# LayerNorm transposes by DMA, a third score bank, a later start of the q and k transposes by DMA, loads on the GpSimd queue, and another order of the first batch

## The chip, the cores and the metric

The kernel runs on one core of a Trainium2 chip. The core has a tensor engine for matrix products (PE, with its weight loads PEld), a vector engine (DVE), an activation engine (ACT), a general engine (GpSimd, POOL) and a queue engine that only starts transfers (SyncE, SP). Each runs its own list of instructions strictly in order and waits for the others by semaphores. Sixteen DMA engines move data; SP, ACT and POOL can each hand them work. The metric is the device time of one execution in microseconds (us); lower is better.

## What is computed

Attention over 8 batches of 12 heads, 448 tokens and 64 columns, with q and k normalised by their root mean square and scaled by g_q and g_k; its output is the input of a LayerNorm and of a two-layer network of width 3072 with a residual:

```python
q_n, k_n = rmsnorm(q, g_q), rmsnorm(k, g_k)
attn = softmax(q_n @ k_n.T / 8)
x = (attn @ v) -> (batch, 448, 768)
xn = (x - mean(x)) / sqrt(var(x) + 1e-6) * g_ln
out = x + relu(xn @ w_ch1) @ w_ch2
```

## The kernel before

Heads go in pairs, six to a batch, 48 in all (pair 0 to 47). Loads and preparation go by **units**: units 0 to 3 are batch 0 (one, one, two and two pairs), and each later batch has three units of two pairs (units 4, 5, 6 are batch 1; unit 7 begins batch 2). A unit's q, k and v come by nine DMAs (L117 and L125) into one of two buffers `qkv`.

The preparation of a unit is cut into pieces that have letters: `a`, `c` square k and q on ACT (L196), `d`, `e` sum the squares on DVE (L199), `g` takes the reciprocal root on ACT (L56, L57), `i` multiplies k by g_q g_k on POOL (L205), `j` rounds it to fp16 on ACT (L213), `k` takes the rest on DVE (L216), `l` scales q on DVE (L63), `m` doubles it, `v`, `w`, `z` convert v on POOL (L262, L268). Then q and k are transposed: up to unit DMA_UNIT by PE into the PSUM bank `tr` or `psQ` and copied by DVE (`K` and `Q` with the pair's number, L290 to L312), from there on by DMA transposes on SP's queue (pieces `x` and `y`, L235 to L248).

`S p.i` is one of seven score steps of a pair: a product of 448 columns on PE (L326, in the last step L329 and L330) and its exponential on ACT (L332), over two PSUM banks. `V p.i` is the matching step of the product with v (L355, L357), and after the seventh DVE divides (L370 to L377). `T` takes LayerNorm's statistics (L499), `A` joins them, `N t` centres one tile of 128 tokens (L519), `X t` transposes it by six PE products and one copy (L546 to L551), `R` is the scale.

The network of a batch is a list of chunks of six products each: 24 of the first layer (psH, L564, with a ReLU on ACT, L566) and, for each tile of 128 tokens, eight of the second (psC, L577, added on DVE, L581). Even batches have three tiles (48 chunks); odd batches also take the left-over tokens of two batches, four tiles (56 chunks).

Batch 0's attention is written out by hand in the table ORDER, which sets the order of every engine there, weight loads included (`W0` to `W4`, converted from fp32 to fp16 by DMAs on POOL's queue, L473 and L478; `L u` is the load of unit u). From then on `run_rest` emits the network of batch b chunk by chunk and lays the attention steps of batch b + 1 between them evenly, so that they end `tail` chunks before the network does; the rest of the chunks has LayerNorm's pieces of batch b + 1 between them. The preparation of a unit is spread over the steps between `st` and `e` in `attention`, the load of the unit after next comes at step `e`.

Of the kernel before, what the change touches and what calls it, by code (L numbers as in the profile page):

```python
# [8 lines left out]
FP32 = mybir.dt.float32  # L9
FP16 = mybir.dt.float16  # L10
INT32 = mybir.dt.int32
ALU = mybir.AluOpType
# [16 lines left out]
DVE_KG, POOL_HI, POOL_DUP, ACT_Q = (0, 1), (1, 2, 3, 4), (1, 2, 4, 5), (0, 1)  # L29
# [6 lines left out]
b0 c0 e0 a0 gq0 d0 b1 i0 G j0 z0 a1 k0 c1 l0 i1 gk0 m0 d1 K0 Q0 e1 b2 g1 a2 l1 j1 d2 m1 S0.0  # L36
S0.1 k1 S0.2 S0.3 L4 W0 L5 K1 c2 e2 S0.4 W1 V0.0 i2 S0.5 Q1 g2 l2 V0.1 j2 S0.6 S1.0 m2 S1.1
S1.2 b3 V0.2 z2 k2 V0.3 S1.3 a3 c3 S1.4 K2 V0.4 V0.5 Q2 V0.6 V1.0 V1.1 S1.5 i3 d3 S1.6 e3 S2.0
V1.2 T0 S2.1 K3 S2.2 S2.3 V1.3 V1.4 z3 S2.4 Q3 W2 V1.5 V1.6 S2.5 S2.6 V2.0 S3.0 g3 S3.1 V2.1
j3 S3.2 W3 W4 S3.3 k3 V2.2 l3 m3 S3.4 K4 b4 Q4 V2.3 a4 V2.4 S3.5 V2.5 V2.6 S3.6 Q5 V3.0 S4.0  # L40
S4.1 K5 c4 V3.1 V3.2 i4 S4.2 S4.3 V3.3 V3.4 V3.5 d4 V3.6 S4.4 S4.5 e4 S4.6 j4 V4.0 V4.1 S5.0
T1 V4.2 k4 g4 S5.1 V4.3 S5.2 V4.4 S5.3 b5 V4.5 l4 z4 m4 G2 L6 S5.4 V4.6 S5.5 a5 V5.0 V5.1 K6
# [29 lines left out]
class _Fast:  # L72


    def __init__(self, ctx, tc, sh, q, k, v, g_ln, w1, w2, out):
        self.g_ln = g_ln
# [26 lines left out]
        self.rr = fix.tile([128, 2, 7 * B * NPAIR], FP32, name="rr_all", tag="rr_all")  # L103
# [23 lines left out]
    def load_first(self):  # L127
# [44 lines left out]
    def pieces(self, u):  # L172
# [9 lines left out]
        def begin():  # L182
# [4 lines left out]
            c["rf"] = self.rr[:, :, o:o + g]  # L187
# [13 lines left out]
        def root(n=slice(0, 2)):  # L201
            _rsqrt(nc, c["rf"][:, n], c["ssq"][:, n], c["rt"][:, n], D * 1e-6)

        def kg():
            (nc.vector if u in DVE_KG else nc.gpsimd).tensor_tensor(  # L205
                out=c["t"][1], in0=c["t"][1],
                in1=sh.gprod.unsqueeze(1).broadcast_to([128, g, D]), op=ALU.mult)
# [11 lines left out]
        def qn():  # L219
            if u < DMA_UNIT:  # L220
                _scaled(nc, c["qn"][:, :, 0], c["t"][0], c["rf"][:, 0])
                return
            x, r = c["t"][0], c["rf"][:, 0]
# [61 lines left out]
    def trans_k(self, p):  # L285
# [3 lines left out]
        kT, ps = self.kU[0][:, 960 * (p % 2):960 * (p % 2) + 960], self.tr  # L289
# [7 lines left out]
    def trans_q(self, p):  # L297
# [5 lines left out]
        qT = self.qU[0][:, p % 2].rearrange("p e s -> p (e s)")  # L303
# [9 lines left out]
        kT = self.kU[0][:, 960 * (p % 2):960 * (p % 2) + 960]  # L313
        self.prs[p] = dict(q=qT, main=kT[:, 192:960], left=kT[:, 0:192])

    def scores(self, p, i):
# [6 lines left out]
        ps = self.ps_s.tile([128, 512], FP32, tag="psS", name="psS")  # L323
# [4 lines left out]
        else:  # L328
# [4 lines left out]
                             scale=self.rr[:, 1, g:g + 1], bias=EXP_BIAS)  # L333
# [53 lines left out]
    def first_attention(self):  # L387
# [7 lines left out]
        for x in ORDER:  # L395
# [7 lines left out]
            elif x == "G2":  # L403
                nc.vector.tensor_scalar(out=gln, in0=gln, scalar1=XS, scalar2=None, op0=ALU.mult)
            elif key == "W":
# [18 lines left out]
    def attention(self):  # L424
# [3 lines left out]
        for u in range(4, nu):  # L428
            p, m = UNIT_PAIR[u], UNITS[u][2]
            st = max(7 * (p - 2 - m) + 2, last + 1, 7 * nb0)  # L430
            e = max(7 * (p - 2) - 1, st + 5)
            pieces = ["bai", "d", "c", "e", "j", "gv", "k", "l", "m", "w", "x", "y"]
            k = len(pieces) - 2
            if u < nu - 2 and f"L{u + 2}" not in done:
                todo.setdefault(e, []).append(lambda u=u: self.load_unit(u + 2))
# [66 lines left out]
    def ln_ops(self, b):  # L502
# [13 lines left out]
        def norm(t):  # L516

            c["xn", t] = self.p_m.tile([128, DM], FP16, tag="xn", name="xn", bufs=3)
# [14 lines left out]
    def ln_list(self, b):  # L533
# [3 lines left out]
        return [call("A", "N0", "N1", "N2", "R")] + [  # L537
            call(f"X{t}", *([f"N{t + 3}"] if t + 3 < n else [])) for t in range(n)]

    def ln_trans(self, b, xn, t):  # L540
        nc, sh = self.nc, self.sh
        if t == 0:
            self.xnT = self.p_m.tile([128, NDC, 512], FP16, tag="xnT", name="xnT")
        ps = self.ps_m.tile([128, NDC, 128], FP16, tag="mlp", name="psX")
# [3 lines left out]
        if b == 0 and t < 2:  # L548
# [75 lines left out]
    def run_rest(self):  # L624
        steps, mark, upto = self.steps, self.mark, self.upto
        tail = 10
# [25 lines left out]
    def flag(self):  # L652
# [5 lines left out]
        good = self.p_m.tile([128, n], FP32, tag="xn", name="good", bufs=3)  # L658
# [5 lines left out]
        nk = self.rr.shape[2]  # L664
        nc.vector.tensor_scalar(out=good[:, 0:nk], in0=self.rr[:, 1], scalar1=sh.gmax,
# [127 lines left out]
def kernel(  # L793
# [21 lines left out]
    gg = sh.w2[:, 0, 0:4 * D].bitcast(FP32).rearrange("p (n d) -> p n d", n=2)  # L815
    nc.scalar.dma_start(gg[:, 0], g_q.unsqueeze(0).broadcast_to([128, D]))
    nc.scalar.dma_start(gg[:, 1], g_k.unsqueeze(0).broadcast_to([128, D]))
    sh.gprod = const.tile([128, D], FP32, name="gprod")
    nc.vector.tensor_tensor(out=sh.gprod, in0=gg[:, 0], in1=gg[:, 1], op=ALU.mult)
    sh.gmax = const.tile([128, 1], FP32, name="gmax")  # L820
    nc.vector.tensor_reduce(out=sh.gmax, in_=sh.gprod, axis=AX.X, op=ALU.max,
                            apply_absolute_value=True)
# [47 lines left out]
```

## Time and profile before

| | |
|---|---|
| median of three runs | 649.29 us (648.17 to 650.2) |
| the profiled execution | 649.09 us, of which the span from first to last instruction is 647.3 |
| PE busy | 594.3 us (92% of the span) |
| ACT, DVE, POOL busy | 362.7, 293.0, 103.1 us |
| granted PE clock, mean | 0.973 |
| moved by DMA | 73.12 MB, on average 113 GB/s |

A busy PE isn't a PE at its peak: products overlap, and a row's time is the time until its results stand. What a product costs is read from the distance between starts.

### The profile page before, as it was taken

To read this page: it belongs to the slowest core of one execution; us is meant where nothing else is said; L and a number is where in the kernel's file an instruction comes from. 1 tells how busy PE (TensorE), PEld (TensorE's weight loads), DVE (VectorE), ACT (ScalarE), POOL (GpSimd) and SP (SyncE) were. 2 spreads that over 40 slices of the span, in tenths; PEclk is the share of its full clock that TensorE was granted. 3 is DMA by queue.
4 is the path that set the end of the run, shared out by engine and by line. 5 is a ranking of instruction groups with operands and counts; after the bars stand their busy time and mean duration, and the time that the engine had idled before them with its cause. 6 is when DMAs were issued, how large, how long until landed. Compare 5 with 4: busy or idle time off the path is not lost.

```text
span 647.3 us, 11504 instructions
## 1 busy us (share of the span) xinstructions
PE 594.3 (92%) x4506; PEld 349.6 (54%) x4506; DVE 293.0 (45%) x633; ACT 362.7 (56%) x673; POOL 103.1 (16%) x116
## 2 busy tenths in 40 slices
PE   2873957999999999999999999999999999999995
PEld 1552534565556666665556666665556666654563
DVE  5795504573425625672434625582443621380011
ACT  5974736644874368635874288626874277314300
POOL 2942310220210202220220111210221100000000
PEclk9996879899999999999999999999999999999998
DMA  8999985554255354564255355455243230010011
GB/s 231 246 220 221 200 178 120 140 140 157 62 141 131 94 130 119 110 151 113 55 133 139 90 132 119 113 140 126 66 107 79 71 62 4 25 50 0 2 50 53
DMA packets 149836, 73.12 MB, mean 113 GB/s; under 512 B 99728, under 2 KB 144784, under 8 KB 149776
## 3 DMA queue, kind: packets, MB, share of 16 engines
q1 hardware_dynamic: 140960, 62.82, 39.4%
q0 software_dynamic: 8528, 9.44, 8.6%
q8 instruction: 37, 0.61, 0.4%
q14 instruction: 23, 0.19, 0.1%
q10 hardware_dynamic: 288, 0.07, 0.0%
HBM read 52.36 MB, written 11.01 MB: 98 GB/s over the span
## 4 chain that ended last, share of the span: by engine, by line
PE 74%; DVE 8%; SPq 7%; DMA 4%; ACT 3%; issue 2%; POOL 0%; ACTq 0%; DVEq 0%; POOLq 0%
PE psH L564 32%; PE psC L577 25%; PE psS L326 7%; PE oA L355 4%; SPq L125 4%; DVE xn L519 3%; DMA qkv<-in_v_dram 2%; PE oB L357 1%; SPq L245 1%; SPq L117 1%; DVE stat L499 1%; PE psX L546 1%; DVE khl L216 1%; ACT E L332 1%; PE psS L329 1%
## 5 line engine op out<-in xcount | busy, mean ns | idle before, releaser
L564 PE MATMUL psH<-xnT,w 128*128 128x512 f16 (+1 forms) x1152 | 250.4, 358 | 0.0
L332 ACT ACTIVATE E<-psS,rr_all 128x448 f16<-128x448 f32 x336 | 207.8, 632 | 71.1 <-PE psS L326 64.6
L577 PE MATMUL psC<-w,hT 128*128 128x384 f16 x1344 | 241.8, 326 | 1.6 <-DVE x L581 1.6
L566 ACT ACTIVATE hT<-psH 128x384 f16<-128x384 f32 (+1 forms) x192 | 105.0, 547 | 132.0 <-PE psH L564 130.8
L577 PEld LDWEIGHTS <-hT 128*128 128x128 f16 x1344 | 124.1, 98 | 72.7 <-issue 2.2
L564 PEld LDWEIGHTS <-w 128*128 128x128 f16 x1152 | 106.0, 99 | 85.1 <-issue 4.7
L326 PE MATMUL psS<-qU,kU 128*128 128x448 f16 x288 | 104.3, 365 | 17.7 <-DMA qU<-qn 10.5
L355 PEld LDWEIGHTS <-E 128*128 128x128 f16 x1008 | 71.6, 99 | 63.9 <-ACT E L332 11.8
L205 POOL TENSOR_TENSOR qkv<-qkv,gprod 128x896 f32<-128x896 f32 x21 | 43.7, 2082 | 325.6 <-issue 253.0
L355 PE MATMUL oA<-v,E 128*128 128x65 f16 x864 | 68.0, 196 | 5.6 <-ACT E L332 5.2
L581 DVE SCALAR_TENSOR_TENSOR x<-psC,rs_all,x 128x384 f32<-128x384 f32 x48 | 29.5, 617 | 85.7 <-PE psC L577 85.1
L199 DVE TENSOR_REDUCE ssq<-khl 128x14 f32<-128x896 f32 (+1 forms) x25 | 26.2, 1048 | 80.1 <-ACT khl L196 80.0
L370 DVE RECIPROCAL rec_all<-oA 128x6 f32<-128x6 f32 x48 | 9.3, 194 | 98.3 <-PE oA L355 98.1
L357 PE MATMUL oB<-v,E 128*128 128x65 f16 x288 | 52.6, 195 | 0.1
L326 PEld LDWEIGHTS <-kU 128*128 128x128 f16 x288 | 28.6, 100 | 36.5 <-issue 17.4
L63 DVE SCALAR_TENSOR_TENSOR qn<-qkv,rr_all 128x256 f16<-128x256 f32 (+2 forms) x81 | 26.9, 393 | 19.9 <-ACT rr_all L57 19.9
L199 DVE TENSOR_REDUCE ssq<-qn 128x14 f32<-128x896 f32 (+1 forms) x25 | 26.1, 1045 | 20.4 <-ACT qn L196 20.4
L357 PEld LDWEIGHTS <-E 128*128 128x128 f16 x336 | 33.0, 98 | 0.6 <-DVE xl L377 0.4
L216 DVE TENSOR_TENSOR khl<-qkv,khl 128x896 f16<-128x896 f32 x21 | 22.8, 1088 | 10.9 <-ACT khl L213 10.9
L372 DVE TENSOR_TENSOR x<-oA,rec_all 128x384 f32<-128x384 f32 x48 | 26.8, 558 | 1.5
L499 DVE BATCH_NORM_STATS2 stat<-x 128x6 f32<-128x256 f32 x72 | 26.1, 415 | 0.7
L262 POOL CAST v<-qkv 128x768 f16<-128x768 f32 x21 | 17.4, 828 | 35.6 <-PE oB L357 19.6
(87 smaller groups left out, 356.9 us busy)
## 6 DMA issues: line engine op xcount, KB each, us to landing
qkv<-in_k_dram SPq DMA_DIRECT2D x21, 384.0 KB, 3.4
qkv<-in_q_dram SPq DMA_DIRECT2D x21, 384.0 KB, 3.9
qkv<-in_v_dram SPq DMA_DIRECT2D x21, 384.0 KB, 4.2
out_dram<-x SPq DMA_DIRECT2D x20, 384.0 KB, 2.5
w<-in_moe_w_ch_dram POOLq DMA_DIRECT2D x3, 1536.0 KB, 20.3
w<-in_moe_w_ch_dram POOLq DMA_DIRECT2D x2, 2304.0 KB, 45.2
qU<-qn SPq DMA_TRANSPOSE x100, 2.4
out_dram<-x SPq DMA_DIRECT2D x8, 192.0 KB, 2.3
```

The source lines that it names most:

```text
L199: nc.vector.tensor_reduce(out=c["ssq"][:, n], in_=c["sq", n], axis=AX.X, op=ALU.add)
L205: (nc.vector if u in DVE_KG else nc.gpsimd).tensor_tensor(out=c["t"][1], in0=c["t"][1], in1=sh.gprod.unsqueeze(1).broadcast_to([128, g, D] ...
L216: nc.vector.tensor_tensor(out=c["khl"][:, :, 1], in0=c["t"][1], in1=c["khl"][:, :, 0], op=ALU.subtract)
L326: nc.tensor.matmul(ps[:, 0:S], c["main"][:, ts(i, 128)], q[:, ts(h, S)], start=True, stop=True)
L332: nc.scalar.activation(out=c["E"][:, i], in_=ps[:, 0:S], func=AFT.Exp, scale=self.rr[:, 1, g:g + 1], bias=EXP_BIAS)
L355: nc.tensor.matmul(oA[:, t, cs], E[:, i, ts(t, 128)], rhs, start=(i == 0 and t == 0), stop=(i == 6 and t == 2))
L357: nc.tensor.matmul(oB[:, cs], E[:, i, 320:448], rhs, start=(i == 0), stop=(i == 6))
L499: nc.vector.bn_stats(out=self.st[b][:, t, 6 * s:6 * s + 6], in_=x[:, 256 * s:256 * s + 256])
L564: nc.tensor.matmul(ps[:, 0:N], sh.w1[:, dc, ts(f, 128)], xnT[:, dc, 0:N], start=(dc == 0), stop=(dc == NDC - 1))
L566: nc.scalar.activation(out=hT[:, f, 0:N], in_=ps[:, 0:N], func=AFT.Relu)
L577: nc.tensor.matmul(ps[:, 0:384], hT[:, f, ts(t, 128)], sh.w2[:, f, ts(g, 384)], start=(f == 0), stop=(f == NFF - 1))
L581: nc.vector.scalar_tensor_tensor(out=x[:, ts(g, 384)], in0=ps[:, 0:384], scalar=self.rs[:, b, t:t + 1], in1=x[:, ts(g, 384)], op0=ALU.mult ...
```

## The change

- ORDER is rewritten and ends with batch 0; the preparation of unit 5 is no longer in it, but between the chunks of batch 0's network. On POOL `W0` stands ahead of unit 1's `j` and `m`, which stood ahead of it.
- The first transfers of k are started on ACT's queue, those of g_q and g_k on SP's. Their product is made in unit 0's piece `i`, and its maximum at `G2`. Unit 2's piece `i` goes from POOL to DVE, unit 5's `m` from POOL to DVE. The reciprocal roots of q and k go to separate tiles, by two instructions in place of one.
- DMA_UNIT is 7 in place of 5: units 5 and 6 (pairs 8 to 11) are transposed by PE.
- From pair 13 on every third score step takes the bank `tr`.
- The load of the unit after next comes one step later, and from unit 9 on (16 units) it is started by POOL.
- LayerNorm's `X` is a DMA transpose of 128 x 768 on SP for batches 1 to 7 (25 tiles), with all of LayerNorm's pieces emitted at once and `tail` 13 in place of 10.

```diff
-DVE_KG, POOL_HI, POOL_DUP, ACT_Q = (0, 1), (1, 2, 3, 4), (1, 2, 4, 5), (0, 1)
+DVE_KG, POOL_HI, POOL_DUP, ACT_Q = (0, 1, 2), (1, 2, 3, 4), (1, 2, 4), (0, 1)
...
-T3 V5.2 V5.3 S5.6 V5.4 V5.5 Q6 V5.6 S6.0 S6.1 S6.2 S6.3 T5 V6.0 z5 A N0 V6.1 V6.2 d5 N1 S6.4
-c5 V6.3 V6.4 i5 j5 X0 S6.5 X1 N2 e5 X2 k5 S6.6 V6.5 g5 l5 m5 x5 V6.6 R y5
+V5.3 V5.4 V5.5 Q6 V5.6 S6.0 S6.1 S6.2 S6.3 T5 S6.4 V6.0 A V6.1 N0 V6.2 N1 V6.3 S6.5 V6.4 X0
+S6.6 V6.5 X1 N2 X2 R V6.6
-DMA_UNIT = 5
+DMA_UNIT = 7
...
+for n, eng in ((0, nc.sync), (1, nc.scalar)):
+    main(eng, n, 0)
+    left(eng, n)
...
+eng = self.nc.sync if u < 9 else self.nc.gpsimd
...
+if p > UNIT_PAIR[DMA_UNIT] and (7 * p + i) % 3 == 2:
+    ps = self.ps_tr.tile([128, 512], FP32, tag="tr", name="psS3")
+else:
+    ps = self.ps_s.tile([128, 512], FP32, tag="psS", name="psS")
...
-e = max(7 * (p - 2) - 1, st + 5)
+e = max(7 * (p - 2) - 1 if u >= DMA_UNIT else 7 * (p - 1) + 1, st + 5)
...
-todo.setdefault(e, []).append(lambda u=u: self.load_unit(u + 2))
+todo.setdefault(e + 1, []).append(lambda u=u: self.load_unit(u + 2))
...
-return [call("A", "N0", "N1", "N2", "R")] + [
-    call(f"X{t}", *([f"N{t + 3}"] if t + 3 < n else [])) for t in range(n)]
+return [call("A", "N0", "N1", "X0", "N2", "X1", *(["N3"] if n > 3 else []), "X2",
+             *(["X3"] if n > 3 else []), "R")]
...
+if b:
+    nc.sync.dma_start_transpose(self.xnT[:, :, ts(t, 128)], xn)
+    return
...
-tail = 10
+tail = 13
```

ACT at the end of batch 0's attention, before. `khl<-qkv`, `qn<-qkv` are the squares and the rounding of unit 5, `xnT` the two copies of LayerNorm, `hT` the network's first ReLU:

```order
L332 ACTIVATE E<-psS,rr_all 128x448 x5
L196 ACTIVATE khl<-qkv 128x896
L332 ACTIVATE E<-psS,rr_all 128x448 x6
L196 ACTIVATE qn<-qkv 128x896
L213 ACTIVATE khl<-qkv 128x14x64
L549 COPY xnT<-psX 128x6x128
L332 ACTIVATE E<-psS,rr_all 128x448
L549 COPY xnT<-psX 128x6x128
```

The same place now:

```order
L344 ACTIVATE E<-psS,rr_all 128x448 x13
L571 COPY xnT<-psX 128x6x128
L344 ACTIVATE E<-psS,rr_all 128x448
L571 COPY xnT<-psX 128x6x128
L57 ACTIVATE stat<-stat 128x3
L58 ACTIVATE rs_all<-stat 128x3
L588 ACTIVATE hT<-psH 128x384
L201 ACTIVATE khl<-qkv 128x896
L588 ACTIVATE hT<-psH 128x384
L201 ACTIVATE qn<-qkv 128x896
L588 ACTIVATE hT<-psH 128x384
L222 ACTIVATE khl<-qkv 128x14x64
```

Unit 5's three instructions moved from ahead of the exponentials and of the copies that the network's first product needs to places behind the network's first three ReLUs.

SP at the end of batch 1's attention, before: the load of a unit, its predecessor's transposes of k and q, then the first stores of batch 0's result.

```order
L117 DMA qkv<-in_q_dram 128x4x192
L125 DMA qkv<-in_q_dram 64x2x64 x2
L117 DMA qkv<-in_v_dram 128x4x192
L125 DMA qkv<-in_v_dram 64x2x64 x2
L235 DMA_TRANSPOSE kU_112<-khl 128x12x128
L238 DMA_TRANSPOSE kU_112<-khl 128x2x64 x2
L245 DMA_TRANSPOSE qU_114<-qn 128x4x128 x3
L248 DMA_TRANSPOSE qU_114<-qn 128x2x64 x2
L605 DMA out_dram<-x 128x384
```

The same place now:

```order
L244 DMA_TRANSPOSE kU_107<-khl 128x12x128
L247 DMA_TRANSPOSE kU_107<-khl 128x2x64 x2
L254 DMA_TRANSPOSE qU_109<-qn 128x4x128 x3
L257 DMA_TRANSPOSE qU_109<-qn 128x2x64 x2
L564 DMA_TRANSPOSE xnT<-xn 128x6x128 x4
L627 DMA out_dram<-x 128x384
```

LayerNorm's four transposes stand behind the unit's own transposes and ahead of the stores, and the load is gone from this queue. On POOL it now stands between one unit's conversion of v and the next unit's piece `i` (L214):

```order
L271 CAST v_111<-qkv 128x12x64
L277 CAST vl<-qkv 64x2x64 x2
L118 DMA qkv<-in_k_dram 128x4x192
L126 DMA qkv<-in_k_dram 64x2x64 x2
L118 DMA qkv<-in_q_dram 128x4x192
L126 DMA qkv<-in_q_dram 64x2x64 x2
L118 DMA qkv<-in_v_dram 128x4x192
L126 DMA qkv<-in_v_dram 64x2x64 x2
L242 MEMSET kU_108 128x2x64
L214 TENSOR_TENSOR qkv<-qkv,gprod 128x896
```

Before, the conversion was followed by the next unit's L205 directly.

More of the change, by code (lines that the diff above doesn't have):

```diff
@@ L201, in root @@
         def root(n=slice(0, 2)):
-            _rsqrt(nc, c["rf"][:, n], c["ssq"][:, n], c["rt"][:, n], D * 1e-6)
+            nc.scalar.activation(c["rt"][:, n], c["ssq"][:, n], AFT.Ln, bias=D * 1e-6)
+            for i in range(2)[n] if isinstance(n, slice) else (n,):
+                nc.scalar.activation(c["r", i], c["rt"][:, i], AFT.Exp, scale=-0.5)
         def kg():
+            if u == 0:
+                nc.vector.tensor_tensor(out=sh.gprod, in0=sh.gg[:, 0], in1=sh.gg[:, 1], op=ALU.mult)
             (nc.vector if u in DVE_KG else nc.gpsimd).tensor_tensor(
@@ L404, in first_attention @@
                 nc.vector.tensor_scalar(out=gln, in0=gln, scalar1=XS, scalar2=None, op0=ALU.mult)
+                gmax = self.sh.gmax
+                nc.vector.tensor_reduce(out=gmax, in_=self.sh.gprod, axis=AX.X, op=ALU.max,
+                                        apply_absolute_value=True)
+                nc.vector.tensor_scalar(out=gmax, in0=gmax, scalar1=1.0 / K_MAX, scalar2=None,
+                                        op0=ALU.mult)
             elif key == "W":
@@ L547, in ln_trans @@
                              start=(dc == 0), stop=(dc == NDC - 1))
-        if b == 0 and t < 2:
+        if t < 2:
             nc.scalar.copy(out=self.xnT[:, :, ts(t, 128)], in_=ps)
```

65 lines of the change are left out of this document (30 added, 35 removed).

## The prediction

> **What bounds the kernel now.** I read the page's span and busy times first, then a table of stretches, then each engine's rows in order of time.
>
> ```profile
> span 647.3 us, 11504 instructions
> 0.00:45.00 45.00, 27.51 (x294) 17.28 (x295) 34.02 (x66) 35.66 (x68) 23.95 (x33) 1.00 1.02 234
> 45.00:66.60 21.60, 8.55 (x81) 5.09 (x78) 12.57 (x27) 9.22 (x17) 4.11 (x5) 0.67 1.22 221
> 66.60:150.00 83.40, 71.28 (x516) 42.48 (x514) 40.64 (x86) 45.78 (x87) 16.63 (x19) 0.90 0.74 155
> 150.00:228.50 78.50, 78.31 (x572) 44.33 (x571) 34.42 (x74) 46.62 (x83) 12.05 (x12) 1.00 0.44 112
> 228.50:293.50 65.00, 63.74 (x530) 39.95 (x528) 35.70 (x78) 43.02 (x83) 11.15 (x12) 1.00 0.56 125
> ```
>
> The columns are length, then busy time of PE, PEld, DVE, ACT and POOL, granted clock, DMA share and GB/s. There are two kernels in one. From 150 us on PE is hardly ever idle and has its full clock: only less PE work helps there. Before that PE is idle for 17.5 us to 45, for 13 us to 66.6 and for 12 us to 150, with a clock of 0.67 and 0.90 in the last two; there the waits decide. I follow the largest.
>
> ```profile
> 50.25 0.95 ACT L196 ACTIVATE khl<-qkv 128x896 f32<-128x896 f32 x1 [5.31 <-DMA qkv<-in_k_dram]
> 58.59 0.88 POOL L262 CAST v<-qkv 128x768 f16<-128x768 f32 x1 [12.96 <-DMA qkv<-in_v_dram]
> 60.47 2.07 POOL L205 TENSOR_TENSOR qkv<-qkv,gprod 128x896 f32<-128x896 f32 x1
> 62.57 0.95 ACT L213 ACTIVATE khl<-qkv 128x896 f16<-128x896 f32 x1 [5.42 <-POOL qkv L205]
> 63.43 0.78 ACT L549 COPY xnT<-psX 128x768 f16<-128x768 f16 x1
> 66.43 2.13 PE L564 MATMUL psH<-xnT,w 128*128 128x384 f16 x6
> PE psS L326 <- DMA qU<-qn: 10.5, 2, 6.5
> PE oA L355 <- ACT E L332: 10.3, 4, 4.7
> ```
>
> Unit 5's data are late because the weight DMAs fill the engines (share 1.22). But nothing of batch 0 needs unit 5: ACT merely stands in order behind its square (5.31 us) and its rounding (5.42 us), which waits for POOL's L205, which stands behind the conversion of v, which waits for v. So the exponentials and the xnT copies are late, PE waits 10.3 us, and the network starts at 66.4. After that PE waits another 10.5 us for two DMA transposes of q, and starts again at about half clock (the six products at 66.43 take 2.13).
>
> **Prices.** From distances between starts, at full clock:
>
> ```profile
> 609.42 31.21 PE psC L577 x192
> 277.71 0.35 PE L326 MATMUL psS<-qU,kU 128*128 128x448 f16 x1
> 277.90 0.26 PE L355 MATMUL oA<-v,E 128*128 128x65 f16 x3
> 278.02 1.14 PE L577 MATMUL psC<-w,hT 128*128 128x384 f16 x6
> 290.76 0.50 PE L546 MATMUL psX<-id,xn 128*128 128x128 f16 x6
> 291.10 1.14 PE L577 MATMUL psC<-w,hT 128*128 128x384 f16 x6
> ```
>
> 192 products of 384 columns in 31.21 us make a chunk of six 0.975; the first layer with three tiles has the same width. A score product is 0.19, a value step 0.12; the last value step of a pair is twice as wide in columns, estimated at 0.2. One LayerNorm tile on PE is 0.34, so 0.057 a transpose, and a `K` or `Q` of seven 0.40.
>
> **Batch 0 and the start of the network.** With unit 5 out of ORDER, ACT goes on after the five exponentials that end at 44.9. The next bound is pair 6's transposes.
>
> ```profile
> 42.18 2.76 ACT L332 ACTIVATE E<-psS,rr_all 128x448 f16<-128x448 f32 x5
> 47.91 0.61 DVE L312 COPY qU<-tr 128x896 f16<-128x896 f16 x1
> 52.32 0.20 DVE L370 RECIPROCAL rec_all<-oA 128x6 f32<-128x6 f32 x1 [3.81 <-PE oA L355]
> 56.85 1.93 DVE L519 SCALAR_TENSOR_TENSOR xn<-x,stat,gln 128x768 f16<-128x768 f32 x2
> ```
>
> That chain ran beside the long wait and stays: Q6's copy ends at 48.5. ACT then has seven exponentials at 0.55 and two copies at 0.7, so 53.8. DVE has, from the division of pair 5 to the last xn, 52.32 to 58.78, less one sum of unit 5 (1.0) that leaves: 5.5, so 54.0, then a transpose (0.34) and its copy (0.6). First network product: **55**, against 66.4. The k transfer that ACT starts and the earlier `W0` shift the first 45 us by at most 1 us, I judge; POOL saves one L205 of 2.1 us there but nothing waited for it. I take nothing, as ACT is the busiest engine there (35.7 of 45) and the second root instruction of each unit gives it some more. The unknown: 53 to 58.
>
> **The network of batch 0.** Work from there to batch 1's first product: 48 chunks 46.8, scores of pairs 7 to 12 (48 products) 9.1, values of 7 to 11 4.6, ten `K` or `Q` 4.0 (eight of them new, in place of DMA transposes): 64.5. LayerNorm's four tiles leave (1.4 before). What stalls it? The loads of units 6 to 8 remain behind the weights.
>
> ```profile
> 55.05 4.04 SPq L125 DMA_DIRECT2D qkv<-in_q_dram  x2
> 71.83 0.95 ACT L196 ACTIVATE qn<-qkv 128x896 f32<-128x896 f32 x1
> w<-in_moe_w_ch_dram POOLq DMA_DIRECT2D x2, 2304.0 KB, 45.2
> 150.07 1.29 PE psH L564 x6
> ```
>
> Unit 6's q is issued until 59.1 and before had landed by 71.8 at the latest, as its square then waited for nothing. The new order wants it about nine chunks and some attention after 55, near 67. So ACT may be late by 0 to 5 us, and DVE behind it in order (the copies of Q8 and K9 stand behind unit 6's sums), part of it hidden by three PSUM banks. Units 7 and 8 can cost as much again; the last weights, issued near 32, land about 45 later and are wanted near 93. With a stretch at half clock I charge **6** (0 to 15). So batch 1's network starts at 55 + 64.5 + 6 = 125.5, in place of 150.1: **24.6** less.
>
> **The later batches.** 21 tiles of batches 2 to 7 at 0.34 leave PE: 7.1. Their DVE copies lay beside PE's chunks. PE's waits from 150 to 577 are these:
>
> ```profile
> PE psX L546 <- DVE x L581: 1.4, 5, 0.4
> PE psC L577 <- DVE x L581: 1.2, 3, 0.4
> PE psS L326 <- ACT E L332: 0.7, 2, 0.3
> ```
>
> The first two belong to the change of batch, where psX takes a bank of the network's, and leave: 2.6. The third is all that a third score bank can save, so I put that at nothing. Loads on POOL: nine issues at 0.88 (row below) and 3 us of its own work (L205, L262) are 11 of the 24 us that a unit lasts (78.5 and 65 us for two batches of three units), and the load stands behind a wait for DVE's `l` that POOL reaches early: hidden. Were it not, piece `i` of the next unit would be late, and ACT's `j` with it.
>
> What is new at the change of batch is a chain with PE behind it: last division, statistics, xn, SP, DMA, first product.
>
> ```profile
> 281.34 0.20 DVE L370 RECIPROCAL rec_all<-oA 128x6 f32<-128x6 f32 x1 [0.65 <-PE oA L355]
> 284.42 2.81 DVE L519 SCALAR_TENSOR_TENSOR xn<-x,stat,gln 128x768 f16<-128x768 f32 x3
> 286.07 2.52 SPq L248 DMA_TRANSPOSE qU<-qn  x2
> qU<-qn SPq DMA_TRANSPOSE x100, 2.4
> DMA to landing us min/median/max: 3.2/4.2/18.9
> 28.85 0.88 POOL L473 DMA_DIRECT2D w<-in_moe_w_ch_dram  x1
> qkv<-in_v_dram SPq DMA_DIRECT2D x21, 384.0 KB, 4.2
> ```
>
> Attention ends at 281.3. The first xn stands at 285.4 and the fourth, no longer behind other work, at 288.2. SP issues a transpose in 1.26 us, so the fourth goes out at 289.2 at the earliest. A shape of 128 x 768 (six blocks of 128 x 128) isn't in the trace: it lies between 2.4 us (four blocks and fewer) and 4.2 (the median of L235, twelve blocks). I take 2.6, near the first: 292. The tail gives 13 chunks, to 294. It just fits, with 2 us to spare, if SP has done with the unit's own transposes; they ended at 288.6 before, but behind a load that leaves this queue. I charge 2.4 us for the seven changes together (0 to 21). Sum: 7.1 + 2.6 - 2.4 = **7.3**.
>
> The Trainium skill, "VectorE: DVE Perf Modes", section "The three transpose paths", speaks against this part: 1309 ns for a block of 128 x 128 by DMA, 390 by TensorE. If blocks went one after another, four tiles of six would take 31 us, each change would come some 20 us late, and seven would cost over 100. Here four blocks land in 2.4 us together, and six blocks on PE cost 0.34: the rows differ from the rule on both sides, and I give it 1 in 100.
>
> **Sum.** 647.3 - 24.6 - 7.3 = 615.4 of span. The profiled execution took 649.09, 1.8 more than its span, and lies at the median of 649.29: **617**.
>
> **Rivals.**
> *Late LayerNorm.* The chain overruns the tail by 1 to 3 us at each of seven changes (POOL's loads now run beside the transposes): 7 to 21 more, about 630. For it: only 2 us of slack, and the row of 4.2. Against it: SP's queue is emptier.
> *The start stays bound by DMA.* The share is 1.22 up to 66.6 whatever the order; if units 6 to 8 stall PE and its clock stays at 0.90, the stalls are 16, not 6: 627. For it: the waits of ACT that leave were waits for DMA at root.
> *Slower: loads by POOL that land late.* A unit's load is wanted 16 steps after its issue, 16 x 1.7 = 27 us (84 steps in 78.5 + 65). Beyond that, with two buffers, every second unit moves all that follows: 16 units, so 8 x (landing - 27). It eats the 32 us gained when a load lands in 31. The weights' row of 45.2 would give 617 + 146 = 763. Against it: that row carries 2304 KB a DMA on full engines; at the later share of 0.44 to 0.56 SP's loads of 384 KB land in 4.2. The Trainium skill, "SBUF — State Buffer", section "SBUF: two separate sides", says that DVE's two-port operations keep GpSimd from writing the descriptors of its DMAs; the issue of 0.88 us above, in a stretch where DVE is busy 34 of 45 us, shows no such delay.
> *Not what it says.* The transposes on PE were hidden after all: 617 + 7 = 624. PE's full rows after 150 speak against it.
>
> **How the numbers follow.** Forecast (606 to 624, the last rival in it) 0.65; late LayerNorm 0.13; start bound by DMA beyond what I charged 0.10; no stalls at all (below 606) 0.06; slower 0.06. The terms' bounds about the forecast are 2 and 3 us (start), 6 and 9 (stalls), 2 and 19 (changes). From below the forecast's own low end to the first two rivals the range is 604 to 632. A measurement tells 0.3% (2 us) from no change. Faster 0.92, same 0.02, slower 0.06.
>
> **What would show it.** The network's first product near 55 and batch 1's near 125; no wait of ACT for unit 5 before the first; PE's waits for qU gone; between the last psC of a batch and the next psH no wait, or, if late LayerNorm is right, one for a DMA of xnT; PE busy after the start lower by about 7 us. The prediction is wrong if POOL's loads land beyond 27 us, or if PE's clock before 125 stays below 0.9.

## The result, and the profile after

The changed kernel takes 628.28 us (median of four runs, 625.77 to 632.25), the kernel before 648.91 (four runs as well): a ratio of 0.9686, with an interval of 0.9629 to 0.9742. That is 20.6 us less. The forecast was 617; 628 lies in the range (604 to 632), but 11 us late, and the three terms of the sum were each off by 5 to 11. Every median below is of undisturbed executions: one of the four of e3 took 1737 us and one of the six of e5 took 884, and both are left out.

First the page's span and busy times, and the same five stretches as before, cut at the new starts of the networks (length, then busy time of PE, PEld, DVE, ACT and POOL, granted clock, DMA share, GB/s). The profiled execution took 629.48.

```profile
span 627.4 us, 11331 instructions
PE 584.6 (93%) x4412; PEld 344.8 (55%) x4412; DVE 286.9 (46%) x612; ACT 362.3 (58%) x697; POOL 194.2 (31%) x258
0.00:45.00 45.00, 25.40 (x263) 15.71 (x264) 32.59 (x62) 33.90 (x68) 20.19 (x29) 1.00 1.02 227
45.00:61.00 16.00, 11.35 (x107) 7.85 (x106) 12.46 (x30) 9.01 (x17) 2.67 (x4) 0.68 1.22 221
61.00:142.50 81.50, 69.85 (x546) 43.26 (x547) 46.98 (x88) 48.72 (x95) 31.77 (x40) 0.94 0.89 157
142.50:219.60 77.10, 77.07 (x552) 43.32 (x553) 32.41 (x70) 46.52 (x86) 29.74 (x39) 1.00 0.61 130
219.60:281.40 61.80, 61.80 (x506) 38.71 (x504) 33.49 (x74) 42.58 (x86) 28.14 (x39) 1.00 0.74 145
```

From 142.5 us on PE has no gap left (77.07 of 77.10, 61.80 of 61.80). In batch 0's network it still stands still for 11.65 us (81.50 less 69.85), about what it was before (12). So the loss against the forecast lies ahead of 142.5.

PE's rows in order of time show the places (start, duration, and in brackets the idle time before it and what ended it; L299 to L316 are now the transposes `K` and `Q`, L338 to L342 the scores, L344 their exponentials, L586 psH, L599 psC, L201 the squares, L225 piece `k`, L304 and L321 the copies of `K` and `Q`, L118 and L126 the loads, L627 the stores, L244 to L257 q's and k's transposes by DMA, L564 the LayerNorm's):

```profile
51.16 0.27 PE L313 MATMUL tr<-id,qn 128*128 128x128 f16 x1 [3.04 <-DVE kU L304]
...
60.97 3.08 PE L586 MATMUL psH<-xnT,w 128*128 128x384 f16 x18 [0.35 <-DVE rec_all L382]
...
101.57 0.53 PE L338 MATMUL psS<-qU,kU 128*128 128x448 f16 x1 [2.25 <-ACT E L344]
...
110.08 0.53 PE L341 MATMUL psS<-qU,kU 128*128 128x448 f16 x1 [4.80 <-ACT E L344]
...
111.22 2.12 PE L599 MATMUL psC<-w,hT 128*128 128x384 f16 x6
...
142.53 1.46 PE L586 MATMUL psH<-xnT,w 128*128 128x512 f16 x6 [1.88 <-DMA xnT<-xn]
```

The first product of the network comes at 60.97 (forecast 55), batch 1's at 142.53 (forecast 125.5). The stop of 4.80 us is paid twice: the six psC products behind it take 2.12 us instead of 1.14, at a granted clock near half.

**The stop at 100 to 115.** PE waits for exponentials. ACT's rows there:

```profile
100.05 0.95 ACT L201 ACTIVATE khl<-qkv 128x896 f32<-128x896 f32 x1 [2.18 <-DMA kU<-khl]
100.90 1.14 ACT L344 ACTIVATE E<-psS,rr_all 128x448 f16<-128x448 f32 x2
108.56 0.95 ACT L201 ACTIVATE qn<-qkv 128x896 f32<-128x896 f32 x1 [6.13 <-DMA qU<-qn]
```

These are the squares of unit 8. They use the tiles khl and qn as scratch, and they wait for transposes *out of* khl and qn: those of unit 7. The two buffers of each tile alternate between units everywhere else, but the program gave unit 8 the tiles that unit 7 had just filled (units 7 and 8 both have khl at address 126848 and qn at 119680; unit 6 has khl at 123264). So ACT stands behind unit 7's eight DMAs, with the exponentials that PE needs behind it. SP's rows say how long those take:

```profile
93.14 1.55 SPq L244 DMA_TRANSPOSE kU<-khl  x1
94.75 2.81 SPq L247 DMA_TRANSPOSE kU<-khl  x2
97.66 3.89 SPq L254 DMA_TRANSPOSE qU<-qn  x3
101.60 2.52 SPq L257 DMA_TRANSPOSE qU<-qn  x2
```

They are issued until 104.1; ACT goes on at 108.56, when the last of them has landed.

**The first product.** DVE's rows around pair 6's transposes, first in the kernel before (L216 is piece `k`, called klo in an expectation below, L404 the scaling of gln, L295 the copy of pair 6's `K`, L499 pair 3's statistics):

```profile
42.30 1.07 DVE L216 TENSOR_TENSOR khl<-qkv,khl 128x896 f16<-128x896 f32 x1
44.29 0.55 DVE L404 TENSOR_SCALAR gln<-gln 128x768 f32<-128x768 f32 x1
...
46.22 0.66 DVE L295 COPY kU<-tr 128x960 f16<-128x960 f16 x1
46.91 1.08 DVE L499 BATCH_NORM_STATS2 stat<-x 128x6 f32<-128x256 f32 x3
```

and now in the changed kernel:

```profile
44.39 1.07 DVE L225 TENSOR_TENSOR khl<-qkv,khl 128x896 f16<-128x896 f32 x1
45.38 1.19 DVE L416 TENSOR_SCALAR gln<-gln 128x768 f32<-128x768 f32 x1
46.49 0.20 DVE L418 TENSOR_REDUCE gmax<-gprod 128x1 f32<-128x64 f32 x1
...
49.33 1.08 DVE L518 BATCH_NORM_STATS2 stat<-x 128x6 f32<-128x256 f32 x3
50.44 0.66 DVE L304 COPY kU<-tr 128x960 f16<-128x960 f16 x1
52.10 0.62 DVE L321 COPY qU<-tr 128x896 f16<-128x896 f16 x1 [1.00 <-PE tr L316]
```

The copy of pair 6's q ends at 52.7. I had taken 48.5 from the trace of before. But piece `k` of unit 4 begins 2.1 us later, though PE's first transpose came at the same time in both traces (10.43 and 10.46); gln's scaling takes 1.19 us instead of 0.55; gmax is new at this place; and pair 3's statistics have moved from behind kU's copy to ahead of it. PE waits 3.04 us for that copy.

That is 4.2 of the 6 us. DVE then needs 5.47 us from the division of pair 5 to the last xn (52.64 to 58.11), as summed up. The rest lies behind the last xn: the first product comes 2.9 us after it, where 0.9 were forecast. From 50.9 to 60.5, behind the stop of 3.04 us, PE's granted clock is 0.50, and the transposes of the LayerNorm stand behind scores and values at that clock. In e6 below, whose longest stop there is 1.1 us, the clock is 1.00 from 50 us on, and the first product comes 1.3 us after the last xn.

### The profile page after: what moved, and what is told of

Same layout as the page of the kernel before. It is cut to its first block, busy times and chain, and to the rows that moved or that the text cites. A ratio compares the mean times of both kernels' runs of the same rounds, so it can differ in the third digit from the quotient of the medians.

```text
span 627.4 us, 11331 instructions
## 1 busy us (share of the span) xinstructions
PE 584.6 (93%) x4412; PEld 344.8 (55%) x4412; DVE 286.9 (46%) x612; ACT 362.3 (58%) x697; POOL 194.2 (31%) x258
## 4 chain that ended last, share of the span: by engine, by line
PE 79%; DMA 8%; DVE 6%; ACT 1%; SPq 1%; issue 1%; POOL 1%; DVEq 0%; ACTq 0%
PE psC L599 32%; PE psH L586 32%; PE psS L338 7%; DMA qkv<-in_k_dram 5%; PE oA L367 4%; DMA qkv<-in_v_dram 2%; PE oB L369 2%; PE psS L341 1%; PE psS L342 1%; DMA qU<-qn 1%; DVE khl L225 1%; DVE qn L64 1%; DVE ssq L204 1%; DVE qU L321 1%; ACT E L344 1%
## 5 line engine op out<-in xcount | busy, mean ns | idle before, releaser
L586 PE MATMUL psH<-xnT,w 128*128 128x512 f16 (+1 forms) x1152 | 245.2, 352 | 2.2 <-DMA xnT<-xn 1.9
L344 ACT ACTIVATE E<-psS,rr_all 128x448 f16<-128x448 f32 x336 | 207.4, 635 | 56.3 <-PE psS L338 50.7
L599 PE MATMUL psC<-w,hT 128*128 128x384 f16 x1344 | 237.3, 328 | 0.0
L588 ACT ACTIVATE hT<-psH 128x384 f16<-128x384 f32 (+1 forms) x192 | 105.6, 550 | 128.6 <-PE psH L586 125.5
L599 PEld LDWEIGHTS <-hT 128*128 128x128 f16 x1344 | 126.9, 98 | 77.4 <-issue 2.5
L586 PEld LDWEIGHTS <-w 128*128 128x128 f16 x1152 | 104.3, 98 | 84.1 <-issue 2.8
L338 PE MATMUL psS<-qU,kU 128*128 128x448 f16 x288 | 102.7, 362 | 9.3 <-ACT E L344 7.9
L367 PEld LDWEIGHTS <-E 128*128 128x128 f16 x1008 | 71.9, 99 | 50.9 <-issue 7.8
L214 POOL TENSOR_TENSOR qkv<-qkv,gprod 128x896 f32<-128x896 f32 x21 | 43.7, 2083 | 86.4 <-ACT khl L201 62.2
L118 POOL DMA_DIRECT2D qkv<-in_k_dram x16 | 12.8, 800 | 141.0 <-ACT E L344 79.2
L338 PEld LDWEIGHTS <-kU 128*128 128x128 f16 x288 | 28.5, 99 | 27.0 <-issue 8.4
L64 DVE SCALAR_TENSOR_TENSOR qn<-qkv,rq 128x256 f16<-128x256 f32 (+2 forms) x75 | 26.8, 415 | 21.0 <-ACT rq L209 21.0
L225 DVE TENSOR_TENSOR khl<-qkv,khl 128x896 f16<-128x896 f32 x21 | 22.7, 1082 | 9.5 <-ACT khl L222 5.7
```

The source lines that it names most:

```text
L64: nc.vector.scalar_tensor_tensor(out=out, in0=x, scalar=8.0, in1=r.unsqueeze(2).broadcast_to([x.shape[0], g, D]), op0=ALU.mult, op1=ALU.mult)
L214: (nc.vector if u in DVE_KG else nc.gpsimd).tensor_tensor(out=c["t"][1], in0=c["t"][1], in1=sh.gprod.unsqueeze(1).broadcast_to([128, g, D] ...
L225: nc.vector.tensor_tensor(out=c["khl"][:, :, 1], in0=c["t"][1], in1=c["khl"][:, :, 0], op=ALU.subtract)
L338: nc.tensor.matmul(ps[:, 0:S], c["main"][:, ts(i, 128)], q[:, ts(h, S)], start=True, stop=True)
L344: nc.scalar.activation(out=c["E"][:, i], in_=ps[:, 0:S], func=AFT.Exp, scale=self.rr[:, g:g + 1], bias=EXP_BIAS)
L367: nc.tensor.matmul(oA[:, t, cs], E[:, i, ts(t, 128)], rhs, start=(i == 0 and t == 0), stop=(i == 6 and t == 2))
```

## The experiments

To compare runs, I take from PE's rows the start of the first psH product of each batch; the differences are the lengths of the networks below. The first transpose on PE (L299) came at 10.4 to 10.5 us in the traces of before and of the changed kernel and at 12.3 to 13.5 in all the experiments. So the first product is counted from it. What comes late there, above all, is g_k, whose load the change had moved to SP's queue, behind q's first: DVE's product of g_q and g_k waits for it for 0.9 to 3.0 us in all twelve experiments, and not at all in the changed kernel's own trace (the load landed in 3.3 us there and in 7.1 in e1).

| kernel | median us | from the first transpose to the first product | batch 0 | batches 1, 3, 5 | 2, 4 | 6 | 7 to the end |
|---|---|---|---|---|---|---|---|
| before | 648.91 | 56.0 | 83.5 | 78.5 | 65.0 | 62.6 | 69.3 |
| changed | 628.28 | 50.5 | 81.6 | 77.1 | 61.8 | 60.6 | 69.4 |
| e1 own slots | 620.14 | 51.1 | 71.6 | 77.1 | 61.8 | 60.6 | 69.6 |
| e2 two banks | 633.98 | 49.2 | 81.5 | 77.4 | 62.9 | 60.6 | 69.5 |
| e3 LN on PE | 640.31 | 49.1 | 80.5 | 78.5 | 64.4 | 63.0 | 69.3 |
| e4 = e1, loads on SP | 643.38 | 48.0 | 79.8 | 78.7 to 79.4 | 67.0, 67.3 | 60.6 | 68.9 |
| e5 = e1, old order | 617.53 | 45.9 | 71.4 | 77.1 | 61.8 | 60.6 | 69.6 |
| e6 = e1, order mended | 618.66 | 47.0 | 72.4 | 77.1 | 61.8 | 60.6 | 69.8 |
| e7 = e1, DMA from unit 5 | 642.46 | 49.4 | 93.5 | 77.1 | 61.8 | 60.6 | 69.4 |
| e8 = e3, two banks | 642.09 | 49.6 | 80.3 | 78.5 | 64.9 | 63.0 | 69.0 |
| e9 = e5, unit 6 later | 615.39 | 46.1 | 71.4 | 77.1 | 61.8 | 60.6 | 69.4 |
| e10 = e3, loads on SP | 634.24 | 50.5 | 72.4 | 78.5 | 64.4 | 63.0 | 69.5 |
| e11 tail 10 | 637.27 | 50.7 | 79.7 | 79.0, 77.4, 77.2 | 63.8, 63.6 | 61.9 | 69.4 |
| e12 = e11, two banks | 638.82 | 50.8 | 81.9 | 79.0, 77.9, 77.2 | 64.0, 64.3 | 61.8 | 69.4 |

The kernel before took 649.25 to 649.48 beside the experiments. The changed kernel was not run again beside them; its ratio's interval (0.9629 to 0.9742) doesn't touch that of any experiment that is compared with it below. The ten kernels with the new order as it was (all but before, e5, e6 and e9) have their first product 48.0 to 51.1 us after the first transpose, 49.9 in the mean: one trace tells such a distance only to about 2 us.

### e1: unit 8 in its own tiles

```diff
-st = max(7 * (p - 2 - m) + 2, last + 1, 7 * nb0)
+st = max(7 * (p - 2 - m) + 2, last + 1, 7 * nb0, 75 * (u == 8))
-c["qn"] = self.p_n.tile([128, 14, 2, D], FP16, tag="qn", name="qn")[:, 0:g]
+c["qn"] = self.p_n.tile([128, 14, 2, D], FP16, tag=f"qn{u % 2}", name="qn", bufs=1)[:, 0:g]
```

(khl likewise. Unit 8 begins three steps later because, in its new tiles, it has to wait for PE's reading of unit 6.)

> The qn and khl tiles of a unit stand in a slot fixed by the unit's parity, and unit 8's preparation begins three steps later, behind pair 11's transposes; all else is as in the changed kernel. Theory (the stalls at 100 to 115 us come from unit 8's squares, which wait for unit 7's transposes by DMA because unit 8 was given unit 7's tiles): ACT's waits of 2.18 and 6.13 us go, PE's of 2.25 and 4.80 with them, and the half clock behind them; batch 1's first product comes at 132 to 135 us instead of 142.5, and the time is 618 to 621. Rival (the transposes of units 7 and 8 are what is late, slowed by the loads that run beside them, whoever waits for them): PE stops at another place for the same time, batch 1's first product stays at 140 to 143, and the time is 626 to 629.

620.14 us, ratio 0.9546 (0.9530 to 0.9563): 8.1 less than the changed kernel, though its first transpose comes 2.6 us later. Batch 0's network is 71.6 us long instead of 81.6. PE's largest waits from the first product to batch 1's (total, times, longest):

```profile
PE psS L341 <- ACT E L344: 4.0, 2, 2.4
PE psH L586 <- DVE rec_all L382: 0.5, 1, 0.5
```

The theory holds: ACT's two waits are gone, and with them 10 us. The rival's row, the landing of k's large transposes, is 7.0 us in the median here and 6.8 in the changed kernel:

```profile
DMA to landing us min/median/max: 3.7/7.0/12.2
```

They are as slow as ever, and nobody waits for them any more. e10 says the same from another side: there unit 8 got the other tiles without any edit for it and without the later start, and batch 0's network took 72.4 (80.5 in e3, from which it differs in the loads alone).

### e2, e3, e8: the third bank and the LayerNorm, apart and together

```diff
-if p > UNIT_PAIR[DMA_UNIT] and (7 * p + i) % 3 == 2:
+if p > B * NPAIR and (7 * p + i) % 3 == 2:
```

> The changed kernel with all scores in the two banks of before. Theory (the third bank is worth what the waits of before showed, 0.7 us): 628 to 629.5. Rival (it is what the later batches gained beyond the LayerNorm's transposes, 2.6 us, or more): 631 to 634, with batch 1's first product unmoved at about 142.5 and the later batches longer.

633.98 us, 5.7 more than the changed kernel. The rival holds. In the traces, 1.4 us is a later first product and lies within the scatter; batches 1 to 7 take 3.2 more (three times 0.3, twice 1.2, before rounding). The only wait of PE from 150 to 520 us is this; the changed kernel has none there. It makes 1.5 of the 3.2; where the rest goes, the waits don't show:

```profile
PE psS L338 <- ACT E L344: 1.5, 4, 0.4
```

e3 undoes the LayerNorm part:

```diff
-if b:
-    nc.sync.dma_start_transpose(self.xnT[:, :, ts(t, 128)], xn)
-    return
...
-tail = 13
+tail = 10
...
-return [call("A", "N0", "N1", "X0", "N2", "X1", ...)]
+return [call("A", "N0", "N1", "N2", "R")] + [call(f"X{t}", ...) for t in range(n)]
```

> The changed kernel with the LayerNorm's transposes of batches 1 to 7 on TensorE again, spread over the last chunks as before (the tail is 10 chunks again, xn keeps its four buffers). Theory (they cost their own TensorE time, 7.1 us, and the 2.6 us of waits at the changes of batch, nothing else): 10 us more than the changed kernel, 636 to 639. Rival (what the later batches gained has another source, the third bank or the score and value products being spaced otherwise): 631 to 634.

640.31 us, ratio 0.9866 (0.9849 to 0.9883). Batches 1 to 6 take 12 us more than in the changed kernel (three times 1.4, twice 2.7, and 2.5): the theory with 2 us on top. e8 is e3 with the edit of e2 too.

> The changed kernel with the LayerNorm's transposes on TensorE and all scores in two banks: the run with LayerNorm on TensorE less the third bank. Theory (the third bank has a price only where the LayerNorm's transposes have left TensorE, since they stood between score products and gave ScalarE time): 0 to 1.5 us above the run with LayerNorm on TensorE, 640 to 642.5, with the later batches at 78.5 and 65.0 us as before. Rival (the two add up): 3 to 5.7 us above it, 644 to 647.

642.09 us; against e3 only batches 2 and 4 grow, by 0.5 each. From batch 1's first product on it takes 497.3 us, the kernel before 497.4: of the whole change only the LayerNorm's way (with its tail) and the third bank show there. With the LayerNorm on PE the third bank is worth 1 us, without it 3.2; the 0.7 us of waits in the trace of before priced the first case, not the second. And the LayerNorm alone, both with two banks (e8 against e2), is worth 3 x 1.1 + 2 x 2.0 + 2.4 = 9.7 us, just the 7.1 + 2.6 of the prediction. (The tail goes with it: 10 chunks in e8, 13 in e2.)

### e4, e10: where the loads are started

```diff
-eng = self.nc.sync if u < 9 else self.nc.gpsimd
+eng = self.nc.sync
```

> As the run with own slots, and all loads of units on SP's queue again. Theory (the loads on GpSimd's queue slow the transposes that run beside them and bring nothing themselves): as the run with own slots or up to 2 us faster, 616 to 621, with the transposes of units 7 to 9 landing in 3 to 5 us instead of 6 to 12. Rival (on SP the loads queue up ahead of the transposes, each of which waits for the DMA eight before it, so q and k come late): 3 to 8 us slower than the run with own slots, with PE waiting for qU or kU.

643.38 us: 23.2 more than e1, three times the rival's upper end. The rival has the queue right and the place wrong: PE waits for xnT above all, and for qU just once (to batch 7's end, from its first product on):

```profile
PE psH L586 <- DMA xnT<-xn: 14.6, 3, 5.3
PE psS L338 <- DMA qU<-qn: 3.1, 1, 3.1
```

The three waits for xnT stand ahead of batches 1, 3 and 5, those of four tiles. SP's rows ahead of batch 3:

```profile
260.29 0.46 SPq L118 DMA_DIRECT2D qkv<-in_k_dram  x1
260.80 1.27 SPq L126 DMA_DIRECT2D qkv<-in_k_dram  x2
...
264.70 3.15 SPq L126 DMA_DIRECT2D qkv<-in_v_dram  x2
267.95 1.47 SPq L244 DMA_TRANSPOSE kU<-khl  x1
...
276.25 2.51 SPq L257 DMA_TRANSPOSE qU<-qn  x2
278.86 0.53 SPq L627 DMA_DIRECT2D out_dram<-x  x1
279.49 5.26 SPq L564 DMA_TRANSPOSE xnT<-xn  x4
```

and PE's first product of that batch:

```profile
286.17 2.29 PE L586 MATMUL psH<-xnT,w 128*128 128x512 f16 x5 [5.01 <-DMA xnT<-xn]
```

The load's nine DMAs hold SP from 260.3 to 267.9; behind them in order stand the unit's transposes until 278.8 and then xnT's. The products wait 5.0 us, and start at a low clock. The transposes themselves do get faster when no load of GpSimd's runs beside them (k's large ones land in 4.5 us in the median, not 7.0), as the theory said, but against what they then stand behind that is worth nothing.

e10 makes the same edit in e3, where xnT doesn't go through SP:

> The run with LayerNorm on TensorE, with all loads of units on SP's queue again (with that, unit 8 also gets tiles of its own, so only the later batches compare). Theory (loads on GpSimd's queue are worth something only where the LayerNorm's transposes stand on SP behind them): later batches of 78.5 and 64.4 us as with loads on GpSimd, 632 to 642 in all. Rival (on SP the loads also hold up q's and k's transposes, as PE's other waits in the run with loads on SP suggest): later batches 1 to 3 us longer each, with PE waiting for qU, 645 to 655.

634.24 us, later batches to the tenth as in e3: the theory holds. Loads on GpSimd are worth nothing there by themselves. They are what lets the LayerNorm's transposes pay: with loads on SP, batches 1 to 6 with the LayerNorm by DMA (e4) are about 5 us *longer* than with it on PE (e10); with loads on GpSimd they are 12 us shorter.

The Trainium skill, "DMA: Bandwidth & Descriptors", section "Issuing engine by pattern", gives plain loads to SyncE and only indirect ones to GpSimd. For the single transfer the rows agree (384 KB land in 3.5 to 4.5 us from SP in e4, in 3.8 to 6.6 from GpSimd in the changed kernel). The order within SP's queue decides here, and by it the path with the slower transfers wins 23 us.

### e5, e6: the order of batch 0

e5 is e1 with the table of before, less unit 5's pieces. e6 is e1 with four places of the new table changed:

```diff
-... d1 c1 W0 K0 Q0 e1 b2 j1 g1 ...
+... d1 c1 K0 Q0 e1 b2 j1 W0 g1 ...
-... z2 V0.3 k2 c3 ...
+... z2 V0.3 k2 G2 c3 ...
-... k4 G2 g4 ... m4 T3 V5.2 K6 S5.6 V5.3 V5.4 V5.5 Q6 V5.6 ...
+... k4 g4 ... m4 V5.2 K6 S5.6 V5.3 V5.4 V5.5 Q6 T3 V5.6 ...
-... X1 N2 X2 R V6.6
+... X1 N2 X2 R V6.6 GM
```

(`GM` is gmax, taken out of `G2`.)

> As the run with own slots, with batch 0's order of before in place of the new one, less unit 5's pieces (they are prepared inside batch 0's network, as in the changed kernel). Theory (what made the first product 6 us later than predicted is the new order itself: W0 ahead of unit 1's cast on GpSimd, and gln, gmax and pair 3's statistics ahead of kU's copy of pair 6 on VectorE): counted from the first transpose on TensorE, the first product comes after 45 to 48 us instead of the 50.5 of the changed kernel and the 51.1 of own slots, and the time is 615 to 618. Rival (VectorE is full from 26 to 58 us, so whatever stands first, the LayerNorm ends when its work is done): 49.5 to 52, and 619 to 622.

> As the run with own slots, with four places of the new order changed: W0 behind unit 1's cast, gln's scaling behind unit 2's klo, pair 3's statistics behind pair 6's q, gmax behind the last copy out of batch 0's attention. Theory (each of these stood on the chain to the first product): counted from the first transpose on TensorE the first product comes after 47 to 49 us, and the time is 616 to 618.5. Rival (VectorE is full, so the order within it is worth nothing but the 0.9 us of gln and gmax): 49.5 to 51, and 619 to 620.5.

617.53 us (ratio 0.9512, 0.9496 to 0.9529) and 618.66 (0.9524, 0.9500 to 0.9549). First product after 45.9 and 47.0 us. In e5, DVE's rows for the same place:

```profile
49.92 0.66 DVE L304 COPY kU<-tr 128x960 f16<-128x960 f16 x1
50.61 1.08 DVE L518 BATCH_NORM_STATS2 stat<-x 128x6 f32<-128x256 f32 x3
51.61 0.61 DVE L321 COPY qU<-tr 128x896 f16<-128x896 f16 x1
```

The copy of q ends 39.0 us after the first transpose (52.22 less 13.25), against 42.3 in the changed kernel and 38.1 in the prediction (48.5 less 10.43). By the rows both lie below the whole scatter of the new order, 4.0 and 2.9 us below its mean; by the medians e5 gains 2.6 us on e1, with intervals that just don't touch, and e6's 1.5 isn't resolved. The theory holds in the main (e6's time is 0.2 us beyond it): DVE was full, but not in the right order. Half to two thirds of the distance shows in the medians. Which of the four places counts isn't separated. `W0` hardly seems to: piece `k` of unit 4 begins 33.8 us after the first transpose in e6, as in the changed kernel (33.9), and 32.2 after it in e5. And what ends PE's stop can change: in e1 it is GpSimd's piece `m` of unit 4, not kU's copy.

### e7: q and k by DMA from unit 5 on

```diff
-DMA_UNIT = 7
+DMA_UNIT = 5
```

> As the run with own slots, with q and k of units 5 and 6 (pairs 8 to 11) transposed by DMA too, so from batch 1's second unit on as before, but with unit 5's pieces inside batch 0's network. Theory (q and k by DMA from batch 2 on only moves 8 transposes of 0.4 us to TensorE, which is full in batch 0's network, and 8 copies to VectorE; it is the taking of unit 5's pieces out of the order that brings the first product forward): batch 0's network 2 to 4 us shorter than the 71.6 us of own slots, 616.5 to 619. Rival (unit 5 must then be ready four pairs earlier and its pieces crowd the network's first steps): scores wait for unit 5's qU or kU, 2 to 8 us slower than own slots, 622 to 628.

642.46 us: 22.3 more than e1, all in batch 0's network (93.5). PE's waits in it:

```profile
PE psS L338 <- DMA qU<-qn: 16.0, 2, 13.6
PE psS L338 <- ACT E L344: 5.8, 3, 5.2
```

The rival holds, at nearly three times its upper end: once unit 5 is prepared inside the network, its transposes by DMA come too late for pair 8 (on SP they stand behind two units' loads, which are issued until 86.1), while those on PE come with the scores. (With DMA_UNIT the third bank also begins four pairs earlier, at pair 9; that isn't separated.) So DMA_UNIT = 7 is no detail of the change: the taking out of unit 5's pieces needs it.

### e9: what is left of batch 0's stops

e5 with unit 6 four steps later:

```diff
-..., 75 * (u == 8))
+..., {6: 55, 8: 75}.get(u, 0))
```

> As the run with own slots and the old order, and unit 6's preparation begins four steps later. Theory (what is left of batch 0's stalls, 3.0 and 1.5 us of PE, is ScalarE standing 2.5 us in unit 6's square of q, whose load lands late beside the weights, with the exps behind it): these waits go, batch 0's network takes 67 to 69 us instead of 71.4, and the time is 614 to 616. Rival (the load is as late for the later square, or unit 6 is then late for pair 10): batch 0's network stays at 71 to 73 us, 617 to 620.

615.39 us (0.9484, 0.9468 to 0.9500), the fastest kernel of the study, 12.9 us below the changed one. But the profiled execution, at 617.6 the slowest of five, has batch 0's network at 71.4 as e5, and ACT's waits in it read:

```profile
ACT khl L222 <- POOL qkv L214: 2.5, 2, 1.9
ACT qn L201 <- DMA qkv<-in_q_dram: 2.1, 1, 2.1
```

The wait for unit 6's q is gone; one for unit 7's q has come in its place, at 87 us. The intervals of e5 and e9 overlap a little. Whether the 2.1 us between the medians come from this edit stays open: the time fell into the theory's range, batch 0's network into the rival's.

### e11, e12: the tail

```diff
-tail = 13
+tail = 10
```

> The changed kernel with a tail of 10 chunks instead of 13 between the end of a batch's attention and the next batch's network. Theory (the chain from the end of attention to the last xnT takes 11 to 11.5 us, 10 chunks take 9.8): PE waits 1.3 to 2.5 us for xnT at each of the six changes from batch 2 on, so that those six batches are longer by that much less what looser attention gives back, and the time is 634 to 643. Rival (the chain shortens when less network work lies beside it): waits below 1 us, 627 to 632.

637.27 us, 9 more than the changed kernel; batches 1 to 7 make 7.4 of it. PE's waits from batch 1's network on:

```profile
PE psH L586 <- DMA xnT<-xn: 4.9, 3, 2.0
PE psH L586 <- DVE good L691: 1.1, 1, 1.1
```

The theory holds for the time, and of its six changes for the three into the batches of four tiles: PE waits 1.6 and 1.3 us for xnT ahead of batches 3 and 5, and 1.1 behind DVE (an instruction of the kernel's closing test) ahead of batch 7. The third wait for xnT, of 2.0 us, stands ahead of batch 1, where the changed kernel has one of 1.9. Into the batches of three tiles it waits for nothing. Batch 1 grows by 1.9 us without a new wait; its clock is 0.76 over the first 7 us (1.00 in the changed kernel), which makes 1.7 of them. e12 has two banks as well:

> As the run with a tail of 10, with all scores in two banks. Theory (with the tail at 13, attention is packed into three chunks fewer, and that density is what gives the third bank its 3.1 us in the later batches): the later batches together lengthen by 0.5 to 1.2 us against the run with a tail of 10. Rival (the LayerNorm's transposes on TensorE were themselves what gave ScalarE time between scores): 2.5 to 3.5 us.

638.82 us; batches 1 to 7 take 1.5 us more than in e11, against 3.2 at a tail of 13. That lies between theory and rival, nearer the theory: about half of what the third bank is worth is due to attention being packed into three chunks fewer. The other half isn't separated.

## Why the prediction was right and wrong

**The bound.** Right: from batch 1 on PE alone counts, and ahead of it waits do. The traces of both kernels fit that reading; with another edit (e4, e11) waits come back at the changes of batch.

**Unit 5 out of ORDER, first product at 55.** The step is right, the place of its end is not. ACT's two waits of 5.3 and 5.4 us are gone. With the old order less unit 5's pieces (e5) the first product comes 45.9 us after the first transpose, against 44.6 forecast and 56.0 before: a gain of 10.1, not 11.4. What failed is the sentence that Q6's chain "ran beside the long wait and stays: Q6's copy ends at 48.5". It was read from a trace with the old order, and the new one had changed DVE's list at that place: the copy ends at 52.7. With it failed the term of at most 1 us for the first 45 (piece `k` was already 2.1 late), and the 0.9 us for the last transpose and its copy, priced at full clock, became 2.9 at half. The 5.5 us gained were 10 from unit 5 less 4 to 5 for the new order (e5 against the changed kernel and against the mean of the ten).

**Batch 0's network, 64.5 of work and 6 of stalls.** The sum was right for a kernel in which unit 8 has its own tiles: 71.6 in e1 (5.0 of it PE's waits), 71.4 in e5, against 70.5. In the changed kernel it was 81.6, and the 10 us are the wait of unit 8's squares for unit 7's transposes. No term of mine covered it: I priced late loads, and took it without a word that the buffers of khl and qn alternate, as they do for every unit of the kernel before. The changed program's own list of waits has it: unit 8's two squares wait for all eight transposes of unit 7, those of unit 7 only for its loads.

**"The start stays bound by DMA" (627).** The number nearly came out (628), the mechanism did not: e1 takes 8 us away without moving a load. Late loads do cost something: PE waits 5.3 and 4.0 us for exponentials in e5 and e9, where ACT waits 2.5 and 2.1 us for a unit's q, and 2.4 and 2.5 for GpSimd. That lies inside the 6 charged.

**The later batches, 7.3.** They gave 12.5 (497.4 us before, 484.9 now). The removal came out to the tenth (9.7 by e8 against e2). The charge of 2.4 for the new chain was not due, but for 1.9 us at batch 1: at batch 3 the last xnT is issued until 278.70 and the next network starts at 281.41. "Just fits" was a fair reading; e11, three chunks shorter, overruns. And the third bank, put at nothing, gave 3.2: its price was taken from waits that stood there with the LayerNorm on PE and a looser attention.

**Loads on GpSimd, hidden.** Right as a cost. The landing times (medians; the longest of any transfer of GpSimd's loads is 11.4 us) also refute the slow rival, which decided at 31 us:

```profile
qkv<-in_k_dram POOLq DMA_DIRECT2D x16, 384.0 KB, 3.8
qkv<-in_q_dram POOLq DMA_DIRECT2D x16, 384.0 KB, 5.0
qkv<-in_v_dram POOLq DMA_DIRECT2D x16, 384.0 KB, 6.6
xnT<-xn SPq DMA_TRANSPOSE x25, 2.5
```

As a worth it was missing: without them the LayerNorm's part would have been a loss of 5 us in batches 1 to 6 and not a gain of 12. I had the condition ("if SP has done with the unit's own transposes; ... a load that leaves this queue") but gave it no price.

**Late LayerNorm (630).** Its number too is near the 628 measured, and its mechanism is refuted but for batch 1's 1.9 us. The transposes of six blocks landed in 2.5 us, where I had taken 2.6.

**Not what it says (624).** Refuted by e3: with the transposes back on PE, PE's busy time rises by 7.4 us (592.0 against 584.6) and the time by 12.0.

The errors cancel only in part: 6 us for the first product and 11 for the network, less 5 for the later batches, make the 12 us of span by which the forecast was early. That 628 lies inside the range is luck in part: the exchanged tiles were no term of the sum, and the third bank was one of nothing. With e5's two edits the kernel takes 617.53, but that it meets the forecast is luck in part too: its first product is 4.1 us late (2.8 of them ahead of the first transpose, by g_k's load), its network 0.9, and the later batches give the 5 back.

## What to carry to other kernels

When a change reorders a program, read the new lists of waits for every tile with few buffers, and compare which buffer each user gets: a single exchange of two slots made ACT stand behind eight DMAs and took 10 of the 30 us that the change could give. A chain priced from the old trace holds only where the new order leaves its engine's list alone. Parts of a change can be worth their sum only together: transposes on an in-order queue pay only if nothing long stands ahead of them there, and a PSUM bank that a trace prices at nothing may be needed once other work is gone from between its users.

## What the runs showed of the hardware

Six blocks of 128 x 128 transposed by one DMA landed in 2.5 us in the median of 25. k's twelve blocks landed in 4.5 us (median, e4) with no load of GpSimd's beside them and in 7.0 (e1) with them. In the changed kernel PE at rest for 4.8 us went on at a granted clock of 0.52 for some 5 us (psC 2.12 us for six, full again at 115.3), and after a rest of 3.0 us it had 0.50 for 9.6 us; after 1.9 us ahead of batch 1 it had 1.00, and in e11, after 2.0 us at the same place, 0.76 over 7 us. The load of g_k (32 KB) landed in 3.3 us in the changed kernel's trace and in 7.1 in e1's, with the same program up to there; why wasn't tried.
